# Reading the token columns of a feed-forward matmul backwards, by a step of minus one

## The chip, the cores and the metric

The kernel runs on one core of one Trainium2 chip. The metric is the device time of one execution in microseconds (us). Before the change the median of three runs is 1150.96 us (1150.13 to 1150.99).

The engines are named as in the profile: PE is TensorE's matmul stream and PEld its weight loads, DVE is VectorE, ACT is ScalarE, POOL is GpSimd, SP is SyncE, which here only issues DMAs.

## The reference

Three parts follow each other; all inputs are float32.

```python
# attention with a sigmoid in place of the softmax: 4 batches, 12 heads, 448 tokens, 64 per head
scores = q @ k.T / sqrt(64) - log(448)
x = sigmoid(scores) @ v                       # as a matrix: 1792 tokens x 768
# layer 1 of the feed-forward part, 768 -> 2048 -> 768
h = x @ w_in
x = (h - tanh(h)) @ w_out
# layer 2, 768 -> 1536 -> 768
out = (sigmoid(x @ w_gate) * (x @ w_val)) @ w_out2
```

## The kernel before

**Layout.** Features lie on the 128 partitions and tokens on the free axis. The 1792 tokens are four batches of 448 (S), one x tile per batch: x0 to x3, each of [128, 2, 6, 448]. The second index tells a value that is rounded to the type F32R (0, "hi") from the remainder (1, "lo"); the third counts the six blocks of 128 features. F32R takes four bytes an element, as F32 does. Weights are kept in the same two parts, in tiles w of [128, 2, 6, 128], decoded from the 64-bit input by ACT, DVE and POOL (`decode`).

**One product.** `mm3` makes one product of a 128x128 weight block with 448 token columns by three matmuls into the same bank of PSUM: w hi with x hi, w hi with x lo, w lo with x hi (lines 228, 229, 230). The token columns are the moving operand, read as a slice `r[:, i, c]` of 448 neighbouring elements on each partition; the weight block is the stationary operand, loaded by an LDWEIGHTS of its own before each matmul. The scores (line 191) and the product with v (line 214) of the attention part don't use `mm3`; the product with v is on plain F32 tiles.

**Loops.** The feed-forward part is a list of 80 steps: 32 of layer 1 (8 groups of two blocks of hidden features, 4 batches each) and 48 of layer 2 (12 blocks, 4 batches each). `hidden_mm(i)` makes the hidden values of a step into a PSUM tile ph, 36 matmuls with x as moving operand. `hidden_act(i)` applies the nonlinearity and leaves the result in an SBUF tile g, again as hi and lo, [128, 2, 2, 448] in layer 1 and [128, 2, 1, 448] in layer 2. `project(i)` multiplies g with the output weights, six blocks d of output features, into PSUM tiles po (36 matmuls a step in layer 1, 18 in layer 2, with g as moving operand), and DVE adds each po to the SBUF accumulator acc (line 328). So 2880 matmuls write ph and 2016 write po, 4896 in all. After layer 1, acc is split into hi and lo and written over x.

**Order.** The schedule is by hand (`tc.manual_schedule`): each engine runs its instructions in the order in which the code emits them. In the loop `hidden_mm(i + 1)` is emitted ahead of `project(i)`, so that PE works on the next hidden values while DVE and ACT make g.

Of the kernel before, what the change touches and what calls it, by code (L numbers as in the profile page):

```python
# [28 lines left out]
def kernel(  # L29
# [12 lines left out]
    nc = tc.nc  # L42
# [182 lines left out]
    later = []  # L225

    def mm3(o, wt, wsl, r, rsl, first, last):
        nc.tensor.matmul(o, wt[(slice(None), 0) + wsl], r[(slice(None), 0) + rsl], start=first, stop=False)  # L228
        nc.tensor.matmul(o, wt[(slice(None), 0) + wsl], r[(slice(None), 1) + rsl], start=False, stop=False)  # L229
        nc.tensor.matmul(o, wt[(slice(None), 1) + wsl], r[(slice(None), 0) + rsl], start=False, stop=last)  # L230

    def plan(i):
        if i < N1:
# [7 lines left out]
    def hidden_mm(i):  # L241
        if i >= NSTEP:
            return
        t, ins, _, _, _ = plan(i)
        ph = psa.tile([128, 2, 512], F32, tag="pa", name=f"ph{i}")
        for j, u in enumerate(ins):
            for c in range(KD):
                mm3(ph[:, j, :S], w_t[u], (c,), x[t], (c,), c == 0, c == KD - 1)
        h_t[i] = ph
# [64 lines left out]
    def project(i, extra):  # L314
# [6 lines left out]
        for d in range(KD):  # L321
            po = psb.tile([128, 512], F32, tag="pb", name=f"po{i}_{d}")
            for j, u in enumerate(outs):
                mm3(po[:, :S], w_t[u], (d,), gt, (j,), j == 0, j == n - 1)
            if first:
                nc.vector.tensor_copy(out=at[:, d], in_=po[:, :S])
            else:
                nc.vector.tensor_tensor(out=at[:, d], in0=po[:, :S], in1=at[:, d], op=ALU.add)  # L328
            if last and i >= N1:
                nc.sync.dma_start(out=out[t, :, d], in_=at[:, d])  # L330
            if extra:
                extra.pop(0)()
# [160 lines left out]
```

## Time and profile before

| what | value |
|---|---|
| median of the runs shown | 1150.96 us |
| the profiled execution, its own time | 1150.52 us |
| its span, from the first to the last instruction | 1148.8 us |
| PE busy | 1140.8 us, 99% |
| PEld busy | 991.5 us, 86% |
| DVE busy | 771.7 us, 67% |
| ACT busy | 459.0 us, 40% |
| POOL busy | 215.3 us, 19% |
| mean granted clock of TensorE | 0.998 of full speed |

The profile gives a matmul a duration from the start of its stream to the end of its result, and the next one starts before that. So the sum of the durations of the matmul rows is more than the span. What a matmul costs in a row of matmuls is the distance from its start to the start of the next one. This document calls that the pitch; it is read from the timeline.

### The profile page before, as it was taken

To read this page: it belongs to the slowest core of one execution; us is meant where nothing else is said; L and a number is where in the kernel's file an instruction comes from. 1 tells how busy PE (TensorE), PEld (TensorE's weight loads), DVE (VectorE), ACT (ScalarE), POOL (GpSimd) and SP (SyncE) were. 2 spreads that over 40 slices of the span, in tenths; PEclk is the share of its full clock that TensorE was granted. 3 is DMA by queue.
4 is the path that set the end of the run, shared out by engine and by line. 5 is a ranking of instruction groups with operands and counts; after the bars stand their busy time and mean duration, and the time that the engine had idled before them with its cause. 6 is when DMAs were issued, how large, how long until landed. Compare 5 with 4: busy or idle time off the path is not lost.

```text
span 1148.8 us, 14490 instructions
## 1 busy us (share of the span) xinstructions
PE 1140.8 (99%) x5865; PEld 991.5 (86%) x5865; DVE 771.7 (67%) x1116; ACT 459.0 (40%) x595; POOL 215.3 (19%) x144
## 2 busy tenths in 40 slices
PE   8999999999999999999999999999999999999998
PEld 4555479999999999999999999999999999999997
DVE  4655646888888888888887856655665655655733
ACT  6888854444444444455555312212212122122210
POOL 0101100011111111111118612222222222222210
PEclk9999999999999999999999999999999999999999
DMA  7555400111111111111110211201201211111004
GB/s 215 161 156 167 128 1 1 56 56 55 55 54 51 46 50 52 53 55 55 56 56 28 83 38 45 83 29 55 82 29 55 72 39 56 59 53 55 28 28 166
DMA packets 24067, 76.44 MB, mean 67 GB/s; under 512 B 3392, under 2 KB 12608, under 8 KB 24000
## 3 DMA queue, kind: packets, MB, share of 16 engines
q1 hardware_dynamic: 23840, 75.28, 20.0%
q8 instruction: 46, 0.75, 0.3%
q10 hardware_dynamic: 160, 0.23, 0.1%
q14 instruction: 21, 0.17, 0.0%
HBM read 69.99 MB, written 5.51 MB: 66 GB/s over the span
## 4 chain that ended last, share of the span: by engine, by line
PE 98%; DVE 1%; DMA 0%; ACT 0%; issue 0%; SPq 0%; DVEq 0%
PE ph L229 17%; PE ph L228 17%; PE ph L230 17%; PE po L229 12%; PE po L230 12%; PE po L228 12%; PE pv L214 7%; PE sa L191 4%; PE sb L191 1%; DVE acc L328 1%; DMA kt<-in_k_dram 0%; ACT at L202 0%; ACT at L196 0%; DVE sp L169 0%; DVE y L263 0%
## 5 line engine op out<-in xcount | busy, mean ns | idle before, releaser
L328 DVE TENSOR_TENSOR acc<-po,acc 128x448 f32<-128x448 f32 x432 | 252.5, 618 | 261.8 <-PE po L230 261.7
L228 PE MATMUL ph<-x,w 128*128 128x448 f32 x960 | 348.6, 363 | 0.0
L229 PE MATMUL ph<-x,w 128*128 128x448 f32 x960 | 348.4, 363 | 0.0
L230 PE MATMUL ph<-x,w 128*128 128x448 f32 x960 | 345.6, 360 | 0.0
L123 POOL TENSOR_TENSOR w<-m,w 128x768 fp32r<-128x768 f32 x68 | 125.5, 1845 | 749.1 <-ACT w L122 736.2
L229 PE MATMUL po<-g,w 128*128 128x448 f32 x672 | 247.0, 367 | 0.0
L230 PE MATMUL po<-g,w 128*128 128x448 f32 x672 | 246.9, 367 | 0.0
L228 PE MATMUL po<-g,w 128*128 128x448 f32 x672 | 246.5, 367 | 0.0
L228 PEld LDWEIGHTS ph<-x,w 128*128 128x128 f32 x960 | 180.1, 188 | 15.3 <-issue 0.7
L230 PEld LDWEIGHTS ph<-x,w 128*128 128x128 f32 x960 | 179.7, 187 | 13.0
L229 PEld LDWEIGHTS ph<-x,w 128*128 128x128 f32 x960 | 180.1, 188 | 10.4
L260 ACT ACTIVATE sg<-ph 128x448 f32<-128x448 f32 x48 | 26.2, 545 | 342.5 <-PE ph L230 342.5
L228 PEld LDWEIGHTS po<-g,w 128*128 128x128 f32 x672 | 125.7, 187 | 12.9
L230 PEld LDWEIGHTS po<-g,w 128*128 128x128 f32 x672 | 125.7, 187 | 12.6
L229 PEld LDWEIGHTS po<-g,w 128*128 128x128 f32 x672 | 125.7, 187 | 12.6 <-POOL g L265 0.2
L96 ACT ACTIVATE m<-st 128x768 f32<-128x768 f32 x68 | 62.0, 911 | 99.8 <-POOL w L123 99.8
L265 POOL TENSOR_TENSOR g<-y,g 128x448 fp32r<-128x448 f32 x48 | 57.9, 1206 | 169.2 <-PE po L230 135.2
L279 ACT ACTIVATE u<-ph 128x896 f32<-128x896 f32 x32 | 29.4, 918 | 129.0 <-PE ph L230 129.0
L214 PE MATMUL pv<-at,vt 112*64 112x448 f32 x384 | 77.2, 545 | 0.0
L196 ACT ACTIVATE at<-sa,bias_s 112x896 f32<-112x896 f32 x72 | 70.4, 1010 | 8.0 <-PE sa L191 7.9
L112 DVE SCALAR_TENSOR_TENSOR m<-st,m 128x768 int32<-128x768 int32 x68 | 67.7, 995 | 2.4
L108 DVE SCALAR_TENSOR_TENSOR m<-st,m 128x768 int32<-128x768 int32 x68 | 67.6, 993 | 1.1
(43 smaller groups left out, 915.4 us busy)
## 6 DMA issues: line engine op xcount, KB each, us to landing
st<-in_w_out_dram SPq DMA_DIRECT2D x28, 768.0 KB, 4.4
st<-in_w_in_dram SPq DMA_DIRECT2D x16, 768.0 KB, 4.5
st<-in_w_gate_dram SPq DMA_DIRECT2D x12, 768.0 KB, 4.4
st<-in_w_val_dram SPq DMA_DIRECT2D x12, 768.0 KB, 4.3
kt<-in_k_dram SPq DMA_DIRECT2D x48, 112.0 KB, 3.1
vt<-in_v_dram SPq DMA_DIRECT2D x24, 224.0 KB, 2.8
out_dram<-acc SPq DMA_DIRECT2D x24, 224.0 KB, 2.2
qt<-in_q_dram SPq DMA_DIRECT2D x46, 112.0 KB, 2.9
```

Source lines behind the costliest of these rows:

```text
L96: nc.scalar.activation(out=mf, in_=hi.bitcast(F32), func=AF.Abs)
L108: nc.vector.scalar_tensor_tensor(out=m, in0=hi, scalar=-0x40000000, in1=m, op0=ALU.bitwise_and, op1=ALU.bitwise_or,)
L112: nc.vector.scalar_tensor_tensor(out=m, in0=lo, scalar=29, in1=m, op0=ALU.logical_shift_right, op1=ALU.bitwise_or,)
L123: nc.gpsimd.tensor_tensor(out=w1, in0=mf, in1=w0.bitcast(F32), op=ALU.subtract)
L191: nc.tensor.matmul(o[j], t[r, kk, c * CP:(c + 1) * CP], t[r, qq], start=(i == 0), stop=(i == 2),)
L196: nc.scalar.activation(out=at[:, :, c], in_=pa[:CP, :, :S], func=AF.Sigmoid, bias=bias_s[:CP], scale=qk_scale,)
L214: nc.tensor.matmul(po[j * D:(j + 1) * D, :S], vt[:, j, c], at[:, j, c], start=(c == 0), stop=(c == NCH - 1),)
L228: nc.tensor.matmul(o, wt[(slice(None), 0) + wsl], r[(slice(None), 0) + rsl], start=first, stop=False)
L229: nc.tensor.matmul(o, wt[(slice(None), 0) + wsl], r[(slice(None), 1) + rsl], start=False, stop=False)
L230: nc.tensor.matmul(o, wt[(slice(None), 1) + wsl], r[(slice(None), 0) + rsl], start=False, stop=last)
L265: nc.gpsimd.tensor_tensor(out=gt[:, 1, 0], in0=y, in1=gt[:, 0, 0].bitcast(F32), op=ALU.subtract)
L328: nc.vector.tensor_tensor(out=at[:, d], in0=po[:, :S], in1=at[:, d], op=ALU.add)
```

## The change

Only `mm3` is touched. Each of the three matmuls now reads its 448 token columns from the last to the first: the moving operand's access pattern starts at element 447 of the slice and has the step minus one. What is written, and the weights, stay as they were.

```diff
     def mm3(o, wt, wsl, r, rsl, first, last):
-        nc.tensor.matmul(o, wt[(slice(None), 0) + wsl], r[(slice(None), 0) + rsl], start=first, stop=False)
-        nc.tensor.matmul(o, wt[(slice(None), 0) + wsl], r[(slice(None), 1) + rsl], start=False, stop=False)
-        nc.tensor.matmul(o, wt[(slice(None), 1) + wsl], r[(slice(None), 0) + rsl], start=False, stop=last)
+
+        hi, lo = (r[(slice(None), i) + rsl + (slice(None, None, -1),)] for i in range(2))
+        nc.tensor.matmul(o, wt[(slice(None), 0) + wsl], hi, start=first, stop=False)
+        nc.tensor.matmul(o, wt[(slice(None), 0) + wsl], lo, start=False, stop=False)
+        nc.tensor.matmul(o, wt[(slice(None), 1) + wsl], hi, start=False, stop=last)
```

Column s of ph now holds token 447 - s. The work between ph and g is element by element, so g holds the tokens backwards too, and the backward read of g in `project` turns them round again: po, acc and the new x are in the order of before. Both programs hold the same instructions with the same waits in the same order on all five engines, and every tile has the same address; in the changed program the 4896 moving operands alone differ, by their start and step. Lines behind 228 are two further down: the matmuls of `mm3` stand at 230, 231 and 232.

## Rows read from the trace of the kernel before

**Rows 1.** The page's head and its first part: busy time, share of the span and instructions of each engine.

```profile
span 1148.8 us, 14490 instructions
PE 1140.8 (99%) x5865; PEld 991.5 (86%) x5865; DVE 771.7 (67%) x1116; ACT 459.0 (40%) x595; POOL 215.3 (19%) x144
```

**Rows 2.** The page's fourth part, the chain of work that ended last, by engine and by line, as shares of the span.

```profile
PE 98%; DVE 1%; DMA 0%; ACT 0%; issue 0%; SPq 0%; DVEq 0%
PE ph L229 17%; PE ph L228 17%; PE ph L230 17%; PE po L229 12%; PE po L230 12%; PE po L228 12%; PE pv L214 7%; PE sa L191 4%; PE sb L191 1%; DVE acc L328 1%; DMA kt<-in_k_dram 0%; ACT at L202 0%; ACT at L196 0%; DVE sp L169 0%; DVE y L263 0%
```

**Rows 3.** The waits of PE in the whole execution: what it waited for, us in total, times, longest.

```profile
PE sa L191 <- ACT sp L165: 1.7, 1, 1.7
PE pz L370 <- DVE z L367: 1.3, 1, 1.3
PE sa L191 <- ACT at L196: 0.5, 1, 0.5
PE sa L191 <- DVE sp L169: 0.4, 1, 0.4
```

**Rows 4.** The page's fifth part, the matmuls of `mm3` and two groups of their weight loads: count, busy us, mean ns of one, idle us before them.

```profile
L228 PE MATMUL ph<-x,w 128*128 128x448 f32 x960 | 348.6, 363 | 0.0
L229 PE MATMUL ph<-x,w 128*128 128x448 f32 x960 | 348.4, 363 | 0.0
L230 PE MATMUL ph<-x,w 128*128 128x448 f32 x960 | 345.6, 360 | 0.0
...
L229 PE MATMUL po<-g,w 128*128 128x448 f32 x672 | 247.0, 367 | 0.0
L230 PE MATMUL po<-g,w 128*128 128x448 f32 x672 | 246.9, 367 | 0.0
L228 PE MATMUL po<-g,w 128*128 128x448 f32 x672 | 246.5, 367 | 0.0
L228 PEld LDWEIGHTS ph<-x,w 128*128 128x128 f32 x960 | 180.1, 188 | 15.3 <-issue 0.7
...
L228 PEld LDWEIGHTS po<-g,w 128*128 128x128 f32 x672 | 125.7, 187 | 12.9
```

**Rows 5.** PE's timeline from 420 to 426 us, in layer 1: start us, duration us, line and operation. Left out are 8 matmuls between the first two rows and 11 between the last two.

```profile
420.09 0.37 PE L228 MATMUL po<-g,w 128*128 128x448 f32 x1
...
421.95 0.37 PE L228 MATMUL po<-g,w 128*128 128x448 f32 x1
...
423.17 0.37 PE L228 MATMUL ph<-x,w 128*128 128x448 f32 x1
...
425.57 0.36 PE L228 MATMUL ph<-x,w 128*128 128x448 f32 x1
```

**Rows 6.** PE's timeline from 1134 to 1149 us, the last two calls of `project`, in the same columns. The last call begins at 1140.77. Left out are 14 matmuls between the first two rows and 13 between the last two.

```profile
1137.67 0.37 PE L228 MATMUL po<-g,w 128*128 128x448 f32 x1
...
1140.77 0.36 PE L228 MATMUL po<-g,w 128*128 128x448 f32 x1
1140.96 0.43 PE L229 MATMUL po<-g,w 128*128 128x448 f32 x1
1141.23 0.36 PE L230 MATMUL po<-g,w 128*128 128x448 f32 x1
1141.43 0.36 PE L228 MATMUL po<-g,w 128*128 128x448 f32 x1
...
1144.23 0.36 PE L230 MATMUL po<-g,w 128*128 128x448 f32 x1
```

**Rows 7.** PE's timeline from 146 to 165 us, around the last product with v: 32 matmuls on plain F32 tiles, which run as 16 pairs, one for each of the two heads, and the matmuls of `mm3` next to them.

```profile
152.48 0.37 PE L230 MATMUL ph<-x,w 128*128 128x448 f32 x1
152.78 6.23 PE L214 MATMUL pv<-at,vt 112*64 112x448 f32 x32
158.94 0.47 PE L228 MATMUL ph<-x,w 128*128 128x448 f32 x1
159.25 0.36 PE L229 MATMUL ph<-x,w 128*128 128x448 f32 x1
```

**Rows 8.** Busy time by stretch, one of layer 1 and one of layer 2: the stretch and its length, then busy us and instructions of PE, PEld, DVE, ACT and POOL, the granted clock, the DMA share and GB/s.

```profile
300.00:430.00 130.00, 130.00 (x642) 119.73 (x641) 110.08 (x144) 63.29 (x71) 16.61 (x9) 1.00 0.15 52
...
700.00:900.00 200.00, 200.00 (x991) 185.21 (x990) 117.10 (x183) 41.50 (x64) 47.10 (x32) 1.00 0.16 55
```

## The prediction

> **What bounds the kernel now.** I read the busy times first, then the chain of work that ended last, PE's waits, the groups of matmuls, and last the timeline, since none of the others gives the price of one matmul. PE is busy for 1140.8 of 1148.8 us [rows 1]. That alone proves little, because a matmul's recorded duration overlaps the next one's: the six groups of `mm3` add up to 1783 us of busy time [rows 4], more than the whole span. The chain settles it. It lies on PE for 98% of the span, and the six groups of `mm3` hold 17 + 17 + 17 + 12 + 12 + 12 = 87% of it [rows 2]. All of PE's waits together are 3.9 us, and they belong to the attention part and the start [rows 3]; the six groups have no idle time ahead of them [rows 4]. So what bounds the kernel is the pitch of 4896 matmuls, 3 x 960 on ph and 3 x 672 on po [rows 4].
>
> The pitch comes from the timeline. On ph 12 matmuls start between 423.17 and 425.57, so 2.40 / 12 = 0.200 us each; on po 9 start between 420.09 and 421.95, so 1.86 / 9 = 0.2067 us each [rows 5]. The sum is 2880 x 0.200 + 2016 x 0.2067 = 576.0 + 416.7 = 992.7 us, 86% of the span, which agrees with the chain's 87%. [...]
>
> **The change part by part.** Removed: nothing. Added: no instruction, no wait, no DMA. Moved: nothing, as the section on the change tells, and so no engine gets its data earlier or later than before relative to the others. What is left is one question, asked 4896 times: does a moving operand that is read at a step of minus one stream at the pitch of one that is read at plus one?
>
> The term is 4896 x (new pitch - old pitch). One nanosecond a matmul is 4896 x 1 ns = 4.9 us, 0.43% of the time. What a measurement of this kernel can tell from no change is about 0.2%, 2.3 us, or 0.47 ns a matmul. So even a small effect would show: there is no cover, since PE waits for nothing in these stages.
>
> [...] From above: the nearest row of a matmul with 448 columns whose stream is slow is the product with v. Its 16 pairs take from 152.78 to 158.94, so 6.16 / 16 = 0.385 us a pair [rows 7], about twice the pitch of `mm3`. Its operands are of another type, so this is a price and not a cause. At that pitch the 4896 matmuls take 4896 x 0.385 = 1885 us, 892 more than now.
>
> Between these ends I take the old pitch, a term of zero. My reason: a slice of x or g is 448 neighbouring four-byte elements, and the reversed read fetches the same bytes from the same addresses once each, neighbour after neighbour. The pitch also doesn't depend on where in SBUF the slice lies: 12 matmuls on eight slices of x keep 0.200 us [rows 5], and the L230 matmuls, which come back to the slice of L228 after another was read, have the same duration as the others within 3 ns [rows 4].
>
> [...]
>
> The sum is 0 us. The profiled execution took 1150.52 us with a span of 1148.8, so 1.7 us lie around the span and don't change; the median of the runs shown is 0.44 us above the profiled execution, and I put the forecast at the median, 1151.
>
> **The rivals.**
>
> First, on the slow side: **the backward stream loses its rate**. If the stage that feeds the array takes two neighbours at a time only where the second lies above the first, a descending stream gives one column where it now gives two. It decides in every one of the 4896 matmuls at once or in none. [...] Against it: nothing in the rows hints that the step's sign matters.
>
> Second, also slower: **ph falls to the pitch of po**. There are two pitches in this trace with the same shapes, weights of the same pool and no waits: 0.200 on x and 0.2067 on g [rows 5]. The step of 6.7 ns isn't tied to g: the last call of `project` starts with 0.2067 behind it (15 matmuls from 1137.67 to 1140.77, 3.10 / 15), is held up once for 0.27 us between 1140.96 and 1141.23, and then runs 14 matmuls on g in 1144.23 - 1141.43 = 2.80, 0.200 each [rows 6]. So the pitch is that of a rhythm between stream and weight load that can lock in one of two ways, and a small shift in when the first column arrives could lock x into the slower one. Price: 2880 x 6.7 ns = 19.3 us, 1170.
>
> Third, faster, by the same mechanism: **po locks into the pitch of ph**. 2016 x 6.7 ns = 13.5 us less, 1137.5. Against both shifts: of the two places on ph and po that I read in the timeline [rows 5, 6], each has the same pitch from one end to the other but for that one stall, so the rhythm is robust where PE isn't held up. DVE would be no new bound: at 110.1 of 130 us busy in layer 1 it has 15% to spare, and in layer 2 over 40% [rows 8], where PE would gain 13.5 / 992.7 = 1.4%.
>
> The weight loads are no rival by themselves. They take 187 to 188 ns [rows 4], below either pitch, and are read as before. That the change doesn't do what it says would be the case if the built program had kept the step of plus one, or had got copies to turn the data round; it has the same number of instructions and the patterns of minus one in it, so I give this nothing.
>
> **How the numbers follow.** No change, 1151: 0.56. The stream loses its rate, about 2043 to 2065: 0.15. ph at the slower pitch, 1170: 0.14. po at the faster pitch, 1137.5: 0.10. The remaining 0.05 is spread over what lies between and beyond: 0.03 for a loss between 1171 and 2043 (a penalty at the start of each stream, or at some of the elements), 0.02 for a gain beyond 13.5 us, down to 1072. Faster by over 0.2%: 0.10 + 0.02 = 0.12. Within 0.2%: 0.56. Slower by over 0.2%: 0.15 + 0.14 + 0.03 = 0.32. The range goes from 1137 to 1171; it holds 0.56 + 0.14 + 0.10 = 0.80 and leaves out the case of the lost rate, which is far away and would stretch it to twice the time.
>
> **What would show it.** If I am right, the timeline of after shows 0.200 us between starts on ph and 0.2067 on po, the six groups of matmuls have means of 360 to 367 ns as before, and the chain has the same shares. If the stream loses its rate, the pitch is near 0.39 us in both groups, the span is near 2040 us, the shares of ph and po in the chain rise to some 92%, and DVE's share of the span falls to under 40%, since its work stays the same. If the rhythm shifts, one group alone moves by 6.7 ns and the other stays. A pitch that is some nanoseconds longer on all 4896 matmuls would mean that the start of each stream is dearer. A change of the granted clock, or new waits of PE, would mean that something is at work that I haven't counted.

## The result and the profile after

The changed kernel takes 1165.33 us (median of 4 runs, 1164.99 to 1165.88) against 1150.79 us for the kernel before (4 runs). The ratio is 1.0129 with a 95% interval of 1.0115 to 1.0142: it is slower by 1.3%, 14.5 us. The profiled execution took 1165.63 us, with a span of 1163.9.

The page's head, its first and its fourth part, and the six groups of `mm3` from the fifth, of the kernel after (answering [rows 1, 2, 4]):

```profile
span 1163.9 us, 14490 instructions
PE 1156.0 (99%) x5865; PEld 993.9 (85%) x5865; DVE 771.3 (66%) x1116; ACT 461.2 (40%) x595; POOL 213.1 (18%) x144
PE 98%; DVE 1%; DMA 0%; ACT 0%; SPq 0%; issue 0%; DVEq 0%
...
L230 PE MATMUL ph<-x,w 128*128 128x448 f32 x960 | 353.6, 368 | 0.0
L232 PE MATMUL ph<-x,w 128*128 128x448 f32 x960 | 353.3, 368 | 0.0
L231 PE MATMUL ph<-x,w 128*128 128x448 f32 x960 | 353.1, 368 | 0.0
...
L230 PE MATMUL po<-g,w 128*128 128x448 f32 x672 | 247.4, 368 | 0.0
L231 PE MATMUL po<-g,w 128*128 128x448 f32 x672 | 247.2, 368 | 0.0
L232 PE MATMUL po<-g,w 128*128 128x448 f32 x672 | 246.1, 366 | 0.0
```

The span grew by 15.1 us, and PE's busy time by 1156.0 - 1140.8 = 15.2. The other engines' busy times differ by 2.4 us at most (PEld). The chain lies on PE as before. The means of the ph groups rose from 360 to 363 ns to 368; those of po stayed near 367. Busy time by stretch shows the same clock, 1.00, and fewer matmuls in the same time, 635 where there were 642 in the first stretch (answering [rows 8]):

```profile
300.00:430.00 130.00, 130.00 (x635) 118.79 (x634) 108.30 (x142) 65.43 (x72) 16.47 (x9) 1.00 0.17 55
700.00:900.00 200.00, 200.00 (x973) 182.38 (x972) 115.12 (x179) 41.69 (x64) 45.38 (x32) 1.00 0.15 52
```

The pitch says the rest. One block of PE's work in layer 1 is 36 matmuls on ph or 36 on po, so the starts of three blocks that follow each other give both pitches, and a start that is rounded to 0.01 us weighs only 0.3 ns of a pitch. PE's timeline of the kernel after, the first matmul of three blocks (start us, duration us; answering [rows 5]):

```profile
411.22 0.37 PE L230 MATMUL ph<-x,w 128*128 128x448 f32 x1
...
418.66 0.37 PE L230 MATMUL po<-g,w 128*128 128x448 f32 x1
...
426.02 0.37 PE L230 MATMUL ph<-x,w 128*128 128x448 f32 x1
```

On ph 7.44 / 36 = 0.2067 us, on po 7.36 / 36 = 0.2044 us. The same reading of the kernel before, at nearly the same time:

```profile
400.49 0.36 PE L228 MATMUL po<-g,w 128*128 128x448 f32 x1
...
407.93 0.36 PE L228 MATMUL ph<-x,w 128*128 128x448 f32 x1
...
415.13 0.36 PE L228 MATMUL po<-g,w 128*128 128x448 f32 x1
```

Here po has 7.44 / 36 = 0.2067 and ph 7.20 / 36 = 0.2000. So ph has lost 0.24 / 36 = 6.7 ns a matmul and po has won 0.08 / 36 = 2.2 ns. The sum is 2880 x 6.7 ns - 2016 x 2.2 ns = 19.3 - 4.4 = 14.9 us, against 15.1 in the span.

### The profile page after: what moved, and what is told of

It is laid out like the page before. It is cut to its first block, busy times and chain, and to the rows that moved or that the text cites. A ratio compares the mean times of both kernels' runs of the same rounds, so it can differ in the third digit from the quotient of the medians.

```text
span 1163.9 us, 14490 instructions
## 1 busy us (share of the span) xinstructions
PE 1156.0 (99%) x5865; PEld 993.9 (85%) x5865; DVE 771.3 (66%) x1116; ACT 461.2 (40%) x595; POOL 213.1 (18%) x144
## 4 chain that ended last, share of the span: by engine, by line
PE 98%; DVE 1%; DMA 0%; ACT 0%; SPq 0%; issue 0%; DVEq 0%
PE ph L230 17%; PE ph L232 17%; PE ph L231 17%; PE po L230 12%; PE po L232 12%; PE po L231 12%; PE pv L214 6%; PE sa L191 4%; PE sb L191 1%; DVE acc L330 1%; DMA kt<-in_k_dram 0%; SPq L146 0%; ACT at L202 0%; ACT at L196 0%; DVE sp L169 0%
## 5 line engine op out<-in xcount | busy, mean ns | idle before, releaser
L230 PE MATMUL ph<-x,w 128*128 128x448 f32 x960 | 353.6, 368 | 0.0
L232 PE MATMUL ph<-x,w 128*128 128x448 f32 x960 | 353.3, 368 | 0.0
L231 PE MATMUL ph<-x,w 128*128 128x448 f32 x960 | 353.1, 368 | 0.0
```

The source lines that it names most:

```text
L230: nc.tensor.matmul(o, wt[(slice(None), 0) + wsl], hi, start=first, stop=False)
L231: nc.tensor.matmul(o, wt[(slice(None), 0) + wsl], lo, start=False, stop=False)
L232: nc.tensor.matmul(o, wt[(slice(None), 1) + wsl], hi, start=False, stop=last)
```

## The experiments

All experiments are read in the same way, by the starts of three blocks in layer 1. Where several runs were made, the ratio is to runs of the kernel before on the same chip (median 1150.69 us). Those with one run stand beside one run of the kernel before, 1150.22 us where nothing else is said. The places in memory that the experiments move are those of the built programs. In the kernel before every slice of x begins at a multiple of 64 bytes (128 past a multiple of 256), and every slice of g 32 past a multiple of 64; a slice is 448 x 4 = 1792 = 28 x 64 bytes long. The weights begin 64 past a multiple of 256. The letters of the theories are those of the recorded expectations, which say what each one forecasts.

**One half at a time.** The step is -1 in `hidden_mm` alone (rev_hidden) or in `project` alone (rev_project). Two layers with one turn each leave the output in order. The edit of rev_hidden against the changed kernel (... stands for lines left out):

```diff
-    def mm3(o, wt, wsl, r, rsl, first, last):
-
-        hi, lo = (r[(slice(None), i) + rsl + (slice(None, None, -1),)] for i in range(2))
+    def mm3(o, wt, wsl, r, rsl, first, last, step=1):
+        hi, lo = (r[(slice(None), i) + rsl + (slice(None, None, step),)] for i in range(2))
...
-                mm3(ph[:, j, :S], w_t[u], (c,), x[t], (c,), c == 0, c == KD - 1)
+                mm3(ph[:, j, :S], w_t[u], (c,), x[t], (c,), c == 0, c == KD - 1, -1)
```

> Only the matmuls on x (ph) read backwards, in both layers; g is read forwards, and layer 2 turns the tokens round again. Theory D (the direction of a matmul's own moving operand sets its pitch): ph 0.2066 us as in the changed kernel, po 0.2066 us as in the kernel before, time 1151 + 2880 x 6.6 ns = 1170 us. Theory L (a rhythm that is carried from one group into the next): po, which now follows a ph in the other rhythm, does not keep 0.2066 us.

Measured: 1156.08 us, ratio 1.0048 (1.0033 to 1.0063). PE's timeline of rev_hidden, the first matmul of three blocks:

```profile
400.59 0.36 PE L229 MATMUL po<-g,w 128*128 128x448 f32 x1
...
407.80 0.37 PE L229 MATMUL ph<-x,w 128*128 128x448 f32 x1
...
415.23 0.36 PE L229 MATMUL po<-g,w 128*128 128x448 f32 x1
```

On ph 7.43 / 36 = 0.2064, as theory D has it. But po, whose instructions, operands and addresses are those of the kernel before, runs at 7.21 / 36 = 0.2003 instead of 0.2067. So theory D is wrong for po, and theory L has its first sign.

> Only the matmuls on g (po) read backwards. Theory D: ph 0.200 us, po 0.2045 us, time 1151 - 2016 x 2.1 ns = 1146.6 us, so faster than both kernels. Theory L: ph does not keep 0.200 us, because it follows a po in another rhythm; then the time is above 1151 us.

Measured: 1146.76 us, ratio 0.9968 (0.9956 to 0.9979), faster than before. PE's timeline of rev_project:

```profile
406.20 0.37 PE L229 MATMUL ph<-x,w 128*128 128x448 f32 x1
...
413.41 0.37 PE L229 MATMUL po<-g,w 128*128 128x448 f32 x1
...
420.77 0.37 PE L229 MATMUL ph<-x,w 128*128 128x448 f32 x1
```

On ph 7.21 / 36 = 0.2003, on po 7.36 / 36 = 0.2044: a backward g has 0.2044 after either kind of ph, and a forward x keeps 0.200 after this po too. Here theory D holds.

**The place instead of the direction.** All reads are forward. In x_plus_32 a pad shifts x by 32 bytes, and a second one brings all that lies behind x, the weights among it, to 64 bytes further on. So it isn't x alone that moves, as the expectation has it. In g_plus_64 a pad moves g down by 32 bytes to a multiple of 64, and with it the scratch tiles of the nonlinearity, which PE doesn't read.

```diff
+    pad0 = xp.tile([128, 8], F32, tag="pad0", name="pad0")
     x = [xp.tile([128, 2, KD, S], F32R, tag=f"x{b}", name=f"x{b}") for b in range(NB)]
+    pad1 = xp.tile([128, 8], F32, tag="pad1", name="pad1")
```

```diff
+                padp = ctx.enter_context(tc.tile_pool(name="padp", bufs=1, side="right"))
+                pad2 = padp.tile([128, 8], F32, tag="pad2", name="pad2")
                 gp = ctx.enter_context(
```

> The kernel before with a pad of 32 bytes ahead of the x tiles and another behind them, so that x alone lies 32 bytes further on; all reads are forward. Theory A (what counts is where in a block of 64 bytes a stream starts: x at 0 has 0.200 us, g at 32 has 0.2066 us): ph goes to 0.2066 us, po stays, 1170 us. Theory D: nothing changes, 1151 us.

Measured: 1166.68 us, ratio 1.0140 (1.0125 to 1.0155). PE's timeline of x_plus_32:

```profile
404.17 0.37 PE L230 MATMUL po<-g,w 128*128 128x448 f32 x1
...
411.57 0.36 PE L230 MATMUL ph<-x,w 128*128 128x448 f32 x1
...
419.00 0.37 PE L230 MATMUL po<-g,w 128*128 128x448 f32 x1
```

On ph 7.43 / 36 = 0.2064 without any backward read: a forward x that begins 32 bytes past a multiple of 64 costs as much as a backward one. Theory A is right on x. Again po moved, to 7.40 / 36 = 0.2056, though g didn't; but the weights did.

> The kernel before with a pad of 32 bytes beyond the g tiles, so that g begins at a multiple of 64 bytes instead of 32 past one; all reads are forward. Theory A: po goes to 0.200 us, ph stays, 1151 - 2016 x 6.6 ns = 1137.7 us. Theory D: nothing changes, 1151 us.

Measured: 1145.57 us, ratio 0.9954 (0.9939 to 0.9969). On po the blocks of g_plus_64 at 398.22, 405.55 and 412.75 give 7.33 / 36 = 0.2036, on ph 7.20 / 36 = 0.2000. The place of g matters, but a multiple of 64 alone doesn't bring it to 0.200; theory A got the sign and half of the size.

**Is a backward read dear because of where it starts?** A slice read backwards starts at its last element, 60 bytes past a multiple of 64. If the start alone counted, x could be moved so that a backward read starts well. In the first two kernels each x tile has 16 elements more and is used from element 1. The 64 bytes more in each tile put the four x tiles at four different places in a block of 256 bytes, where they had shared one, and the weights 256 bytes further on.

```diff
-    x = [xp.tile([128, 2, KD, S], F32R, tag=f"x{b}", name=f"x{b}") for b in range(NB)]
+    x = []
+    for b in range(NB):
+        xw = xp.tile([128, 2 * KD * S + 16], F32R, tag=f"x{b}", name=f"x{b}")
+        x.append(xw[:, 1:1 + 2 * KD * S].rearrange("p (i c s) -> p i c s", i=2, c=KD))
```

> The kernel before with x four bytes further on, so that each forward read of x starts 4 past a multiple of 64 bytes. Theory S (a stream that starts at a multiple of 64 bytes has 0.200 us, any other start 0.2065 us, whatever the direction): ph at 0.2065 us, time 1156 to 1170 us by what po does. If only a shift by half a block costs: ph stays at 0.200 us.

Measured: one run, 1168.95 us. PE's timeline of x_plus_4, five blocks:

```profile
397.00 0.37 PE L231 MATMUL ph<-x,w 128*128 128x448 f32 x1
...
404.55 0.37 PE L231 MATMUL po<-g,w 128*128 128x448 f32 x1
...
411.98 0.37 PE L231 MATMUL ph<-x,w 128*128 128x448 f32 x1
...
419.46 0.36 PE L231 MATMUL po<-g,w 128*128 128x448 f32 x1
...
426.68 0.37 PE L231 MATMUL ph<-x,w 128*128 128x448 f32 x1
```

On ph 7.55 / 36 = 0.2097 and 7.48 / 36 = 0.2078: four bytes cost more than the forecast 6.5 ns. And po takes 7.43 / 36 = 0.2064 in one step and 7.22 / 36 = 0.2006 in the next, in one execution and with g forward in both. Two pitches of the same kind of block stand side by side here. They follow a pattern: from 165 us on both pitches repeat every four steps, one for each x tile (on po in layer 1 0.2064, 0.2006, 0.2067 and 0.2001), so po, whose own operand g doesn't move, goes with the x tile of the step.

> The kernel with ph alone backwards, with x four bytes further on, so that each backward read starts at byte 448 x 4 = 1792 of its slice's block, a multiple of 64, and not 60 past one. Theory S: ph is back at 0.200 us. Theory D (the direction costs by itself): ph stays at 0.2065 us.

Measured: one run, 1156.62 us. PE's timeline of rev_x_plus_4:

```profile
407.71 0.37 PE L232 MATMUL ph<-x,w 128*128 128x448 f32 x1
...
415.15 0.37 PE L232 MATMUL po<-g,w 128*128 128x448 f32 x1
...
422.36 0.37 PE L232 MATMUL ph<-x,w 128*128 128x448 f32 x1
```

On ph 7.44 / 36 = 0.2067. Theory S has fallen: a backward read that starts at a multiple of 64 bytes isn't cheaper than one that starts 60 past it (0.2064 in rev_hidden). On po 7.21 / 36 = 0.2003, as in rev_hidden.

> The kernel with ph alone backwards, with x 32 bytes further on, so that each backward read starts 28 past a multiple of 64 bytes. Theory S: ph at 0.2065 us, no change against ph alone backwards. Theory D with an own cost for the place: ph above 0.2065 us, near 0.213 us, since direction and place would add up.

The pad is that of x_plus_32. Measured: one run, 1164.84 us. Blocks at 404.04 (po), 411.43 (ph) and 418.87 give 7.44 / 36 = 0.2067 on ph and 7.39 / 36 = 0.2053 on po. Direction and place don't add up: each alone has 0.2064 on ph (rev_hidden, x_plus_32), and the sum would be near 0.213. In layer 2, ph has two pitches in alternate steps, with x always at the same place in a block of 256 bytes: from 744.73 to 752.16 it takes 7.43 / 36 = 0.2064, from 755.86 to 763.21 7.35 / 36 = 0.2042. So x can have more than one pitch at one place too. The time differs from rev_hidden by 8.7 us mostly for po, 5.0 ns x 2016 = 10 us, less what ph wins in those steps.

**What is the bound, columns or weights?** The second and third matmul of each product stream 384 columns, so the kernel leaves out two of the three terms for 64 tokens of each batch (the two lines of 448 columns that these replace aren't shown).

```diff
+        cut = slice(0, 384)
...
+        nc.tensor.matmul(o[:, cut], wt[(slice(None), 0) + wsl], r[(slice(None), 1) + rsl + (cut,)], start=False, stop=False)
+        nc.tensor.matmul(o[:, cut], wt[(slice(None), 1) + wsl], r[(slice(None), 0) + rsl + (cut,)], start=False, stop=last)
```

> The kernel before; the second and third matmul of each product stream 384 columns in place of 448 (64 tokens of each batch lose two of their three terms), weight loads and all else stay. If the stream of columns is the bound, the start of the next matmul comes 64 / 2.4 = 26.7 ns earlier after each of these two: ph 0.200, 0.173, 0.173 us. If the weight load of 187 ns with its hand-over is the bound, the pitch stays at 0.190 us or above.

Measured: one run, 1052.76 us. PE's timeline of cols_384 on ph, four matmuls that follow each other:

```profile
421.41 0.36 PE L229 MATMUL ph<-x,w 128*128 128x448 f32 x1
421.61 0.33 PE L230 MATMUL ph<-x,w 128*128 128x384 f32 x1
421.78 0.34 PE L231 MATMUL ph<-x,w 128*128 128x384 f32 x1
421.95 0.36 PE L229 MATMUL ph<-x,w 128*128 128x448 f32 x1
```

The pitches are 0.20, 0.17 and 0.17. The whole block, from 420.86 to 427.42, gives 6.56 / 36 = 0.1822 us in the mean, 17.8 ns below 0.2000. The 0.64 us less than the 7.20 of the kernel before fall on 24 shortened matmuls: 0.64 / 24 = 26.7 ns for 64 columns, 0.4167 ns a column. The expectation had this number from a rate that no run had shown before. The weight loads have not become shorter (from the page of cols_384):

```profile
L230 PEld LDWEIGHTS ph<-x,w 128*128 128x128 f32 x960 | 180.5, 188 | 0.0
```

A pitch of 0.17 us is below these 188 ns. So the stream of columns is the bound on ph here, and not the weight load. By estimate from this rate, 448 columns take 448 x 0.4167 = 186.7 ns, and 13.3 of the 200.0 ns come on top. On po the block from 414.30 to 420.86 gives the same 0.1822: the 6.7 ns that po takes above ph in the kernel before are gone, with g where it was.

**Does po remember how it was entered?** A matmul of 16 columns of zeros, with a weight load of its own, is put behind the first matmul of each call of `project` (the call, which sets `kick`, isn't shown).

```diff
         nc.tensor.matmul(o, wt[(slice(None), 0) + wsl], r[(slice(None), 0) + rsl], start=first, stop=False)
+        if kick:
+            nc.tensor.matmul(o[:, :16], z[:, :128], z[:, :16], start=False, stop=False)
```

> The kernel before, all reads forward, plus one matmul of 16 columns of zeros behind the first matmul of each call of project (80 in all; it adds nothing to the result). It disturbs the rhythm in which po is entered and nothing else. Theory L (po keeps the rhythm into which it was pushed; both 0.200 and 0.2065 us are stable): the pitch on po behind it is no longer 0.2065 us, most likely 0.200 us, and the time is 1151 - 2016 x 6.5 ns + 80 x 0.1 us = 1146 us. Theory P (the pitch on po is set by its own addresses): po stays at 0.2065 us, 1151 + 8 = 1159 us. ph stays at 0.200 us by both.

Measured: 1150.16 us, ratio 0.9995 (0.9985 to 1.0004): no difference in time, but not for want of an effect. PE's timeline of kick_po, one block on po and the start of the next on ph:

```profile
413.94 0.37 PE L228 MATMUL po<-g,w 128*128 128x448 f32 x1
414.15 0.18 PE L230 MATMUL po<-z 128*128 128x16 bf16 x1
414.19 0.45 PE L231 MATMUL po<-g,w 128*128 128x448 f32 x1
414.47 0.37 PE L232 MATMUL po<-g,w 128*128 128x448 f32 x1
...
415.29 0.36 PE L228 MATMUL po<-g,w 128*128 128x448 f32 x1
...
421.29 0.37 PE L228 MATMUL ph<-x,w 128*128 128x448 f32 x1
```

From 415.29 to 421.29 there are 30 matmuls on g in 6.00 us, 0.2000 each, with g where it always was. So at these addresses theory L is right and theory P wrong: one small disturbance at its entry sets the pitch of the block behind it. The first six matmuls with the added one take 415.29 - 413.94 = 1.35 us where six at 0.200 take 1.20, so a kick costs 0.15 us, 80 x 0.15 = 12 us, and that eats the gain of 2016 x 6.7 ns = 13.5 us. I had put 0.1 us for it.

**A better place for g.** The pad of g_plus_64 has 24 elements instead of 8: g then begins 128 past a multiple of 256 bytes, where x begins.

> The kernel before with a pad of 96 bytes beyond the g tiles, so that g begins at 128 past a multiple of 256 bytes, as x does; all reads forward. Theory A2 (the place in a block of 256 bytes counts, and x has a good one): po goes to 0.200 us, 1137.7 us, faster than all kernels so far. Theory L: po takes some pitch between 0.200 and 0.2066 us, as it did at a multiple of 64 (0.2037 us).

Measured: 1137.40 us, ratio 0.9882 (0.9867 to 0.9897), faster than both kernels and all others but cols_384, which leaves out part of the sums. PE's timeline of g_plus_96:

```profile
411.23 0.36 PE L228 MATMUL po<-g,w 128*128 128x448 f32 x1
...
418.43 0.36 PE L228 MATMUL ph<-x,w 128*128 128x448 f32 x1
...
425.63 0.36 PE L228 MATMUL po<-g,w 128*128 128x448 f32 x1
```

Both blocks take 7.20 / 36 = 0.2000. This is what theory A2 forecast, within 0.3 us.

> The kernel before with x, and all that lies behind it in SBUF (the weight tiles too), 64 bytes further on; reads forward. If the place of x in a block of 64 bytes is what counts, ph stays at 0.200 us and the time near 1151 us. If blocks of 128 or 256 bytes count, or the place of the weights, ph goes to 0.2065 us, as it did with x 32 bytes further on (there the weights moved by 64 bytes too).

The pad ahead of x has 16 elements and there is none behind it. Measured: one run, 1147.99 us, beside a median of 1150.69 for the kernel before on that chip. PE's timeline of x_plus_64:

```profile
400.05 0.37 PE L229 MATMUL po<-g,w 128*128 128x448 f32 x1
...
407.44 0.36 PE L229 MATMUL ph<-x,w 128*128 128x448 f32 x1
...
414.64 0.37 PE L229 MATMUL po<-g,w 128*128 128x448 f32 x1
```

On ph 7.20 / 36 = 0.2000, on po 7.39 / 36 = 0.2053. So x is as good at 64 bytes further, though it now lies 192 past a multiple of 256, and the shift of the weights by 64 bytes isn't what slowed ph in x_plus_32. On po it may well count: in x_plus_32, rev_x_plus_32 and here, the three runs with the weights (and all else behind x) 64 bytes further on, po has 0.2053 to 0.2056, whether ph has 0.2064, 0.2067 or 0.2000. No run moved the weights alone.

> The kernel before with only the second matmul of each product on ph (the one on x lo) backwards, so that its term lands on the wrong tokens; only the time is looked at. If each backward stream costs 6.5 ns by itself: mean pitch on ph 0.200 + 6.5 / 3 = 0.2022 us. If one backward stream in three is enough to push the whole group into the slower rhythm: 0.2065 us. If a change of direction from one matmul to the next costs: above 0.2065 us.

Only the second matmul of each product on ph, the one on x lo, reads backwards, so its term lands on the wrong tokens. Measured: one run, 1147.70 us, beside the same 1150.69. Blocks at 405.58 (ph), 412.90 (po) and 420.12 give 7.32 / 36 = 0.2033 on ph and 7.22 / 36 = 0.2006 on po. One backward stream in three costs 3.3 ns in the mean, that is half of what three cost and more than the third that independent streams would cost. None of the three forecasts holds: the cost is neither one of each stream by itself nor one of the whole group. Again po has left 0.2067, as in rev_hidden, with nothing of its own changed.

## Why the prediction was right or wrong

**The bound was right.** PE's pitch is the kernel's time: 14.9 us from two pitches explain the 15.1 us of the span, and cols_384 shows that the columns set it on ph, by 26.7 ns for 64 of them.

**The step that failed is the term of zero** in "The change part by part". It rested on two reasons. The first, that the same bytes are read from the same addresses, was true and didn't suffice: rev_hidden and rev_x_plus_4 show that a backward x has 0.2064 to 0.2067 us where a forward one has 0.2000. The second, that the pitch doesn't depend on where a slice lies, was a reading error. The eight slices that I had compared all begin at a multiple of 64 bytes, so they could not show it; x_plus_32 gives 0.2064 and x_plus_4 0.2078 to 0.2097 for forward reads. Nor did durations that agree within 3 ns show anything: the prediction itself puts what can be told at 0.47 ns a matmul.

**The second rival is what happened.** It had 0.14: ph falls to the pitch of po, 2880 x 6.7 ns = 19.3 us, 1170. The pitch on ph became 0.2067, what it had named within the 0.3 ns of the reading, and the term measured 19.3. rev_hidden shows what did it: the direction of the reads of x alone moves ph there. What the rival left out is that po would move the other way at the same time, by 2.2 ns, 4.4 us; rev_project gives a backward g the same 0.2044 with ph at 0.2003. That was the third rival in part; I had treated the two as exclusive. The time lies inside the stated range because of these two, which it was drawn to hold; for the forecast in its middle that was luck.

**The objection to both was wrong.** I argued from [rows 5, 6] that the rhythm is robust where PE isn't held up. For x that is nearly so: with forward reads from a multiple of 64 bytes ph came to 0.200 in all six kernels whose blocks I read that way (before, rev_project, g_plus_64, kick_po, g_plus_96, x_plus_64), whatever po did between. For g it isn't: with the same forward instructions on g and every tile at its old address, po ran at 0.2067 (before), 0.2003 (rev_hidden), 0.2006 (rev_lo_only) and at 0.2000 behind a kick. The other moves of po, in x_plus_32, rev_x_plus_32, x_plus_64 and x_plus_4, came with the weights or the x tiles at other places, so they can't be put down to the entry alone. The hold-up in [rows 6], after which po ran at 0.200, was the first sign of this. It is shorter than I wrote: 0.27 us is the distance of two starts, some 0.07 more than a pitch. And I had read it as a rhythm with two pitches, where po took at least five: 0.200, 0.2036, 0.2044, 0.2053 and 0.2067.

**The first rival fell.** No stream lost its rate; the largest pitch of a block read above is 0.2097 us, against the 0.39 that this rival needs. How many elements the array is fed at a time is shown by no run; that was a guess of mine. The 2065 us among the chances, and the 1072 at the other end, take 186.7 ns for a set of 448 columns, the second as the least that a matmul can take. No run shows that least. In its place cols_384 shows 26.7 ns for 64 columns, which gives the 186.7 ns as an estimate, and the lowest pitch read on `mm3` with 448 columns is 0.2000 us.

**What stays open.** Why a backward stream or one 32 bytes further on costs some 6.5 ns, one 4 bytes further on up to 9.7, and why direction and shift together cost no more, isn't settled: the runs show the sizes and not the mechanism, nor that the weight load has a part in it, as the second rival had it. What moved po where the weights moved too is open as well. Nor is it shown whether g_plus_96 is good because of g's place or because that place lets po lock into the better rhythm; g at another multiple of 64 had 0.2036, while x is good at two such places. A backward read of g at the place of g_plus_96 wasn't tried, nor the weights at another place with all else as it was.

## What to carry to other kernels

When PE is busy without waits, price its matmuls by the distance between starts in the timeline, find what the columns take of it by a run with fewer of them (here 26.7 ns for 64, in cols_384), and compare the pitch of each kind of operand; here 0.2000 against 0.2067 us in the kernel before was worth 1.2%, and a pad of 96 bytes won it (g_plus_96). Before saying that an access pattern's place or direction doesn't matter, check that the rows compared differ in it. A few nanoseconds on each of thousands of matmuls can change in a group that wasn't edited (po went from 0.2067 to 0.2003 us in rev_hidden), so read the pitch of every group after an edit, and not only of the one touched.

## What I had not expected of the hardware

- With the same 448 columns, weights of the same size and a mean granted clock of 0.998 to 1.00, the pitch of `mm3` took values between 0.2000 and 0.2097 us by the direction of the read (from 0.2000 on ph to 0.2064 in rev_hidden), by where in SBUF the moving operand lies (from 0.2000 on ph to 0.2064 in x_plus_32 and 0.2097 in x_plus_4, from 0.2067 on po to 0.2000 in g_plus_96), and by how a block was entered (from 0.2067 on po to 0.2000 in kick_po). The lowest is 13.3 ns above the 186.7 ns of the columns, which are an estimate from the 26.7 ns for 64 columns in cols_384. No block of `mm3` with 448 columns in each matmul that I read came under 0.2000 us.
- The pitch of a block can depend on how it was entered: one matmul of 16 columns moved 30 matmuls behind it from 0.2067 to 0.2000 us (kick_po).
- A matmul pitch of 0.17 us held with a weight load of 188 ns ahead of each matmul (cols_384). The 36 loads of a block are 36 x 188 ns = 6.77 us, and the block takes 6.56, so a load can be recorded as still under way when the next one starts.
